# Low parts of weights: GpSimd's subtraction replaced by a negated copy on ScalarE and an adding DMA

## The chip, the cores and the metric

The kernel runs on one core of a Trainium2 chip. The metric is the device time of one execution in microseconds (us). The core's engines work side by side, each through its own queue in order: TensorE (PE in the rows; PEld is its weight load), VectorE (DVE), ScalarE (ACT), GpSimd (POOL) and SyncE (SP), which only issues DMAs. ScalarE and GpSimd can issue DMAs too.

## The reference

Linear attention with learned features, then two stacks of dense products. The second and third stage are what matters here:

```python
def _moe_ref(x, w_a, w_b, w_out):                    # x 1152x512, w_a and w_b 512x1536, w_out 1536x512
    return ((x @ w_a) * (x @ w_b)) @ w_out

def _moe2_ref(x, domain_probs, w1, w2):              # 4 experts, w1 512x1024, w2 1024x512 each
    p = domain_probs / (domain_probs.sum(-1, keepdims=True) + 1e-09)
    out = 0
    for e in range(4):
        out += p[:, e:e + 1] * (np.maximum(x @ w1[e], 0.0) @ w2[e])
    return out
```

Before that, phi(x) = exp of plus and minus (x @ w_phi less its largest magnitude); keys and values give sums per head, queries divide them out.

## The kernel before

TensorE multiplies in a rounded 32-bit format (float32r). To keep precision, each operand is cut into a high part, the rounded value, and a low part, what rounding took away; each product is then three matmuls: high by high, high by low, low by high. The low part of the *weight* is read by the third matmul of a product with stationary weights (lines 602, 686, 716, 743 and 772) and by the second where the weight moves (line 818).

**Where low parts are made.** `two_parts` (line 108): ScalarE rounds the source into `hi` (line 109), then GpSimd subtracts `hi` from the source into `lo` (line 110). It is called in two places, 116 times in all.
- `parts` (line 449), for the first MLP, 36 times, 128x512. Its weights (`ab` for the two inner products, `o` for the outer) come as 64-bit numbers. `begin` (ScalarE: two copies), `middle` (VectorE: lines 436, 439, 442; GpSimd: an integer addition, line 445) make 32-bit values in a tile `wx` of two buffers, and `parts` cuts them into `w`.
- `parts_w` (line 497), for the second MLP, 16 units of five calls. A unit ("1", j) has seven 256-column slices, made of sums of the loaded weights by a scheme that saves products (`sums_w`, GpSimd); they are cut in calls of 768, 512 and 512 columns into `wc`, of which there are two in turn. A unit ("2", j) has two calls of 512 columns into `w`.

**What sets the order.** The tasks `begin`, `middle`, `parts`, `load_w`, `sums_w` and `parts_w` stand in one list. `prep(n)` runs the next n of them, as long as the buffer that they write has had its last reader in program order; `need(u)` runs all that a unit of weights still lacks. During attention a string (`SCRIPT`, letter w) says where a task is run; after it `run` gives so many tasks for each step of matmuls. Nothing else moves them: each engine goes through its queue in the order of the program.

**Stages on the time line of the profile.** Attention to about 93 us; the first MLP, which begins inside it at 81 us, to about 328 us (units of 288 tokens, in its middle blocks of 384); then the second MLP, whose first unit begins between the first's last ones, in a regular pattern of about 24 us for each j from 346 us to the end.

Two lines are needed word for word. A product with the weight's low part in the third matmul, and the wait that VectorE's write of `wx` implies, since that tile has two buffers:

```python
nc.tensor.matmul(out=ps, lhsT=wlo, rhs=xhi, start=False, stop=a == 1, skip_group_check=True)     # line 602
x = w_p.tile([128, 512], U32, tag="wx", name="wx", bufs=2)                                       # line 434
```

Of the kernel before, what the change touches and what calls it, by code (L numbers as in the profile page):

```python
# [12 lines left out]
AF = mybir.ActivationFunctionType  # L13
ALU = mybir.AluOpType
# [40 lines left out]
def tile_linear_attention_then_mlps(ctx, tc, qT, kT, v, w_phi, wab, wout, w12, probs, out):  # L55
    nc = tc.nc
# [40 lines left out]
    with tc.manual_schedule():  # L97
# [10 lines left out]
        def two_parts(hi, lo, src, eng):  # L108
            nc.scalar.activation(out=hi, in_=src, func=AF.Copy)  # L109
            eng.tensor_tensor(out=lo, in0=src, in1=hi.bitcast(F32), op=ALU.subtract)  # L110

        NC = 6 * 128
        xraw = {}
# [300 lines left out]
        w_t = {}  # L414
        state = {}
# [33 lines left out]
        def parts(k):  # L449
            u, f = f64[k]  # L450
            if u in SPARE:
                if u not in w_t:
                    t = m_p.tile([128, 2, 2, 2, 512], F32R, tag="xc", name="w")
                    w_t.update((s, t[:, i]) for i, s in enumerate(SPARE))
            elif f == 0:
                p, n = (ab_p, 4) if u[0] == "ab" else (od_p, 2)
                w_t[u] = p.tile([128, 2, 2, 512], F32R, tag=u[0], name="w", bufs=n)
            two_parts(w_t[u][:, 0, f], w_t[u][:, 1, f], state.pop(k), nc.gpsimd)

        stage_t = {}  # L460

# [35 lines left out]
        def parts_w(u, lo, hi):  # L497
            def go():
                if u[0] == "1":
                    w_t[u] = wc_t[u[1] % 2]  # L500
                    src = stage_t[u][0][:, 1:4] if lo == 0 else stage_t[u][1][:, lo - 3:hi - 3]
                else:
                    src = stage_t[u][:, lo:hi]
                    if lo == 0:
                        w_t[u] = od_p.tile([128, 2, 2, 512], F32R, tag="o", name="w", bufs=2)
                two_parts(w_t[u][:, 0, lo:hi], w_t[u][:, 1, lo:hi], src, nc.gpsimd)
            return go


# [2 lines left out]
        for k in range(NW + 2):  # L512
            if k >= 2:
                tasks.append((f64[k - 2][0], lambda k=k: parts(k - 2), f64[k - 2][1] == 0))
            if 1 <= k <= NW:
                tasks.append((f64[k - 1][0], lambda k=k: middle(k - 1), False))
            if k < NW:
                tasks.append((f64[k][0], lambda k=k: begin(k), False))
# [261 lines left out]
        def unit_h(j, tp):  # L780
            c = new_c("h")

            def parts(src, f, lo, hi):
                free_hh(tp)
                nc.scalar.activation(out=hh_of(tp, f, 0, lo, hi), in_=src, func=AF.Relu)  # L785
                nc.vector.scalar_tensor_tensor(  # L786
                    out=hh_of(tp, f, 1, lo, hi), in0=src, scalar=0.0, in1=hh_of(tp, f, 0, lo, hi).bitcast(F32),
                    op0=ALU.max, op1=ALU.subtract,
                )

            def last(X):
                parts(X, 1, HT, 2 * HT)
                rows = range(4) if tp == 0 else range(4, 9)
                (queue if j + tp else kept).extend(
                    (pos[0] + (4 if j + 1 == tp else 3), ((0, 0, S), (1, 0, S)) if i == 4 else ((tp, 0, S),), lambda i=i: o2(j, i))
                    for i in rows
                )

            return unit(
                ("1", j), tp, c, lambda: parts(c[:, 0], 0, 0, 2 * HT), lambda: parts(c[:, 1, :HT], 1, 0, HT), last  # L800
            )
# [225 lines left out]
```

## Time and profile before

| | |
|---|---|
| median of 3 runs | 705.61 us (705.39 to 706.54) |
| the profiled execution, whole | 705.69 us |
| its span (first to last instruction) | 703.8 us |
| TensorE busy | 694.3 us, 99% |
| VectorE busy | 413.2 us, 59% |
| ScalarE busy | 295.5 us, 42% |
| GpSimd busy | 274.5 us, 39% |
| DMA, mean | 65 GB/s, 46.04 MB |

Times in rows count from the start of the span. A busy share is an average over the whole span and says nothing of a single stage; idle time of an engine on which nobody waits costs nothing. A matmul's row shows its start and a modelled end; neighbours overlap, so the distance of starts is what one costs. What an engine waited for is inferred from semaphores.

### The profile page before, as it was taken

What the parts mean: (1) busy time and instruction counts of PE and PEld (TensorE: products, weight loads), DVE (VectorE), ACT (ScalarE), POOL (GpSimd) and SP (SyncE); (2) the same over time, 40 slices, a digit from 0 to 9 for tenths busy, and PEclk for the clock granted to TensorE, in tenths of its full rate; (3) what the DMA queues carried; (4) which work ended last, traced back from release to release, by engine and by line L of the source; (5) the groups of instructions that cost most, each with busy time, mean ns of one, the idle gap of its engine ahead of it and who ended that gap; (6) DMA issues with size and microseconds to landing.
All of it is one profiled execution on the core that took longest, in us unless ns stands there. A gap on an engine that the chain in (4) does not pass through costs nothing.

```text
span 703.8 us, 13086 instructions
## 1 busy us (share of the span) xinstructions
PE 694.3 (99%) x5202; PEld 638.3 (91%) x5202; DVE 413.2 (59%) x721; ACT 295.5 (42%) x595; POOL 274.5 (39%) x242
## 2 busy tenths in 40 slices
PE   9998999999999999999999999999999999999998
PEld 8995689999999999999889898989898889888987
DVE  6899865657665565636345555555545554545454
ACT  6677855354434443335633243333323332333221
POOL 2222564334434437331763534353435243524200
PEclk9999999999999999999999999999999999999999
DMA  7641222313232321121221110211022101100003
GB/s 211 193 143 51 77 74 65 86 61 98 89 84 90 90 70 53 61 61 31 61 73 47 61 31 31 61 60 31 31 61 56 34 31 61 47 15 0 1 1 136
DMA packets 47966, 46.04 MB, mean 65 GB/s; under 512 B 5584, under 2 KB 39952, under 8 KB 47904
## 3 DMA queue, kind: packets, MB, share of 16 engines
q1 hardware_dynamic: 47648, 45.00, 21.5%
q8 instruction: 41, 0.67, 0.4%
q14 instruction: 21, 0.17, 0.1%
q10 hardware_dynamic: 224, 0.16, 0.1%
q0 software_dynamic: 32, 0.03, 0.0%
HBM read 42.81 MB, written 2.36 MB: 64 GB/s over the span
## 4 chain that ended last, share of the span: by engine, by line
PE 92%; DVE 5%; issue 1%; ACT 0%; POOL 0%; SPq 0%; DVEq 0%; ACTq 0%
PE acc L819 10%; PE acc L818 9%; PE acc L817 9%; PE X L600 5%; PE X L601 5%; PE X L602 5%; PE kv L237 5%; PE ab L685 4%; PE ab L684 4%; PE ab L686 4%; PE acc L715 2%; PE Z L600 2%; PE acc L716 2%; PE Z L601 2%; PE acc L714 2%; PE Z L602 2%
## 5 line engine op out<-in xcount | busy, mean ns | idle before, releaser
L827 DVE SCALAR_TENSOR_TENSOR oacc<-acc,pr,oacc 128x512 f32<-128x512 f32 (+1 forms) x136 | 101.4, 746 | 116.8 <-PE acc L819 116.8
L110 POOL TENSOR_TENSOR w<-wx,w 128x512 fp32r<-128x512 f32 x68 | 90.2, 1327 | 157.5 <-ACT w L109 157.5
L819 PE MATMUL acc<-w,hhb 128*128 128x512 f32 x290 | 114.1, 394 | 0.0
L818 PE MATMUL acc<-w,hhb 128*128 128x512 f32 x290 | 113.4, 391 | 0.0
L110 POOL TENSOR_TENSOR wc<-wt,wc 128x512 fp32r<-128x512 f32 (+1 forms) x48 | 69.9, 1482 | 110.3 <-ACT wc L109 110.0
L817 PE MATMUL acc<-w,hhb 128*128 128x512 f32 x290 | 112.9, 389 | 0.0
L445 POOL TENSOR_TENSOR wx<-wx,rn 128x512 uint32<-128x512 uint32 x36 | 46.4, 1289 | 95.9 <-DVE wx L442 95.9
L600 PE MATMUL X<-xc,wc 128*128 128x288 f32 x256 | 77.0, 301 | 0.7 <-ACT h L605 0.5
L785 ACT ACTIVATE hhb<-h 128x288 fp32r<-128x288 f32 x64 | 36.2, 565 | 98.2 <-DVE h L608 98.2
L601 PE MATMUL X<-xc,wc 128*128 128x288 f32 x256 | 75.8, 296 | 0.0
L685 PE MATMUL ab<-xl,w 128*128 128x288 f32 x256 | 75.5, 295 | 0.2 <-POOL xl L338 0.2
L684 PE MATMUL ab<-xh,w 128*128 128x288 f32 x256 | 75.6, 295 | 0.0
L686 PE MATMUL ab<-xh,w 128*128 128x288 f32 x256 | 75.4, 295 | 0.0
L602 PE MATMUL X<-xc,wc 128*128 128x288 f32 x256 | 75.4, 295 | 0.0
L605 ACT ACTIVATE h<-X 128x288 f32<-128x288 f32 x64 | 26.0, 406 | 108.5 <-PE X L602 108.4
L819 PEld LDWEIGHTS acc<-w,hhb 128*128 128x128 f32 x290 | 54.4, 188 | 14.0 <-DVE hhb L786 2.8
L786 DVE SCALAR_TENSOR_TENSOR hhb<-h,hhb 128x288 fp32r<-128x288 f32 x64 | 39.6, 618 | 42.2 <-ACT hhb L785 42.2
L818 PEld LDWEIGHTS acc<-w,hhb 128*128 128x128 f32 x290 | 54.4, 188 | 8.3
L817 PEld LDWEIGHTS acc<-w,hhb 128*128 128x128 f32 x290 | 54.5, 188 | 7.8
L608 DVE TENSOR_TENSOR part<-acc,part 128x288 f32<-128x288 f32 (+2 forms) x80 | 34.6, 451 | 33.4 <-PE acc L772 19.9
L600 PEld LDWEIGHTS X<-xc,wc 128*128 128x128 f32 x256 | 48.0, 188 | 4.3 <-ACT h L605 0.7
L601 PEld LDWEIGHTS X<-xc,wc 128*128 128x128 f32 x256 | 48.2, 188 | 2.7
(105 smaller groups left out, 1629.2 us busy)
## 6 DMA issues: line engine op xcount, KB each, us to landing
raw<-in_wab SPq DMA_DIRECT2D x192, 64.0 KB, 2.0
wt<-in_w SPq DMA_DIRECT2D x64, 128.0 KB, 2.4
wx<-in_w SPq DMA_DIRECT2D x32, 256.0 KB, 3.0
raw<-in_wout SPq DMA_DIRECT2D x12, 512.0 KB, 3.7
xraw<-in_qT SPq DMA_DIRECT2D x6, 384.0 KB, 3.4
v<-in_v SPq DMA_DIRECT2D x8, 256.0 KB, 4.6
out<-oacc SPq DMA_DIRECT2D x8, 256.0 KB, 2.0
xraw<-in_kT SPq DMA_DIRECT2D x4, 384.0 KB, 5.1
```

The costliest lines, as they stand in the source:

```text
L110: eng.tensor_tensor(out=lo, in0=src, in1=hi.bitcast(F32), op=ALU.subtract)
L445: nc.gpsimd.tensor_tensor(out=x, in0=x, in1=r, op=ALU.add)
L600: nc.tensor.matmul(out=ps, lhsT=whi, rhs=xhi, start=first and a == 0, stop=False, skip_group_check=True)
L601: nc.tensor.matmul(out=ps, lhsT=whi, rhs=xlo, start=False, stop=False, skip_group_check=True)
L602: nc.tensor.matmul(out=ps, lhsT=wlo, rhs=xhi, start=False, stop=a == 1, skip_group_check=True)
L684: nc.tensor.matmul(out=t, lhsT=whi, rhs=hi, start=(c == 0), stop=False)
L685: nc.tensor.matmul(out=t, lhsT=whi, rhs=lo, start=False, stop=False)
L686: nc.tensor.matmul(out=t, lhsT=wlo, rhs=hi, start=False, stop=(c == KD - 1))
L817: nc.tensor.matmul(out=acc, lhsT=hi, rhs=whi, start=f == 0, stop=False)
L818: nc.tensor.matmul(out=acc, lhsT=hi, rhs=wlo, start=False, stop=False)
L819: nc.tensor.matmul(out=acc, lhsT=lo, rhs=whi, start=False, stop=f == 1)
L827: nc.vector.scalar_tensor_tensor(out=o, in0=acc, scalar=sc, in1=o, op0=ALU.mult, op1=ALU.add)
```

## The change

`two_parts` stays, and nothing calls it any more. A new function takes its place at both calls. ScalarE rounds into `hi` as before, then writes the rounded value with its sign turned into `lo`; a DMA that GpSimd issues adds the source onto `lo`. So `lo` is again source minus rounded value. Seven lines come in at line 111, so line numbers of the changed kernel below it are higher by seven.

```diff
+        def two_parts_dma(hi, lo, src):
+
+
+            nc.scalar.activation(out=hi, in_=src, func=AF.Copy)
+            nc.scalar.activation(out=lo, in_=src, func=AF.Copy, scale=-1.0)
+            nc.gpsimd.dma_start(out=lo, in_=src, accum_op=ALU.add)
...
-            two_parts(w_t[u][:, 0, f], w_t[u][:, 1, f], state.pop(k), nc.gpsimd)
+            two_parts_dma(w_t[u][:, 0, f], w_t[u][:, 1, f], state.pop(k))
...
-                two_parts(w_t[u][:, 0, lo:hi], w_t[u][:, 1, lo:hi], src, nc.gpsimd)
+                two_parts_dma(w_t[u][:, 0, lo:hi], w_t[u][:, 1, lo:hi], src)
```

The queues of the built programs show what moved, at three places.

ScalarE's queue at the change-over to the second MLP, before. `wc` is the unit ("1", 1), `w` the unit ("2", 1), `wt` and `wx` their loaded sources; the lines between are copies out of PSUM:

```order
L605 ACTIVATE h<-X 128x288
L109 ACTIVATE wc<-wt 128x768
L605 ACTIVATE h<-Z 128x288
L785 ACTIVATE hhb<-h 128x288
L109 ACTIVATE wc<-wt 128x512
L785 ACTIVATE hhb<-h 128x576
L785 ACTIVATE hhb<-X 128x288
L109 ACTIVATE wc<-wt 128x512
L605 ACTIVATE h<-X 128x288
L109 ACTIVATE w<-wx 128x512 x2
```

And in the changed program:

```order
L612 ACTIVATE h<-X 128x288
L115 ACTIVATE wc<-wt 128x768
L116 ACTIVATE wc<-wt 128x768
L612 ACTIVATE h<-Z 128x288
L792 ACTIVATE hhb<-h 128x288
L115 ACTIVATE wc<-wt 128x512
L116 ACTIVATE wc<-wt 128x512
L792 ACTIVATE hhb<-h 128x576
L792 ACTIVATE hhb<-X 128x288
L115 ACTIVATE wc<-wt 128x512
L116 ACTIVATE wc<-wt 128x512
L612 ACTIVATE h<-X 128x288
```

Behind each rounding stands its negated copy (line 116), ahead of the copies that came next; nothing else changed its place.

GpSimd's queue in the first MLP's first weights, with its waits, before (`xl` is the low part of the input x, `rn` the rounding term of the 64-bit numbers):

```order
L110 TENSOR_TENSOR w<-wx,w 128x512 [waits Activation_49]
L445 TENSOR_TENSOR wx<-wx,rn 128x512 [waits DVE_49]
L338 TENSOR_TENSOR xl<-x,xh 128x576 [waits Activation_49]
L110 TENSOR_TENSOR w<-wx,w 128x512 [waits Activation_49]
L445 TENSOR_TENSOR wx<-wx,rn 128x512 [waits DVE_49]
```

And changed:

```order
L117 DMA w<-wx 128x512 [waits Activation_49,Pool_49]
L452 TENSOR_TENSOR wx<-wx,rn 128x512 [waits DMASW4_49,DVE_49]
L345 TENSOR_TENSOR xl<-x,xh 128x576 [waits Activation_49]
L117 DMA w<-wx 128x512 [waits Activation_49,Pool_49]
L452 TENSOR_TENSOR wx<-wx,rn 128x512 [waits DMASW5_49,DVE_49]
```

Each subtraction became a DMA at the same place. The addition to `wx` now also waits for the landing of an earlier adding DMA (DMASW is the completion of a DMA that GpSimd issued), that of two weights before, which read the same buffer; VectorE's write of `wx` (line 442, now 449) waits for it too, in place of a subtraction.

TensorE's queue where the second MLP's unit ("1", 0) begins, with its waits, before:

```order
L600 MATMUL X<-xc,wc 128x288 [waits Activation_49]
L601 MATMUL X<-xc,wc 128x288 [waits DVE_49]
L602 MATMUL X<-xc,wc 128x288 [waits Pool_49]
L600 MATMUL X<-xc,wc 128x288 [waits Activation_49]
L601 MATMUL X<-xc,wc 128x288 [waits DVE_49]
```

And changed:

```order
L607 MATMUL X<-xc,wc 128x288 [waits Activation_49]
L608 MATMUL X<-xc,wc 128x288 [waits DVE_49]
L609 MATMUL X<-xc,wc 128x288 [waits DMASW5_49]
L607 MATMUL X<-xc,wc 128x288 [waits Activation_49]
L608 MATMUL X<-xc,wc 128x288 [waits DVE_49]
```

The order is the same; the first matmul that reads a low part waits for a DMA's completion in place of GpSimd. So it is for all 116 low parts.

## Rows read from the trace of the kernel before

**Rows 1.** The page: busy time by engine, and the chain that ended last.

```profile
PE 694.3 (99%) x5202; PEld 638.3 (91%) x5202; DVE 413.2 (59%) x721; ACT 295.5 (42%) x595; POOL 274.5 (39%) x242
...
PE 92%; DVE 5%; issue 1%; ACT 0%; POOL 0%; SPq 0%; DVEq 0%; ACTq 0%
```

**Rows 2.** Busy time in a stretch; columns as in its first line.

```profile
core 0: us, PE busy (x) PEld busy (x) DVE busy (x) ACT busy (x) POOL busy (x), PEclk, DMA share, GB/s
47.00:680.00 633.00, 628.65 (x4352) 576.16 (x4349) 363.42 (x634) 259.74 (x526) 262.76 (x227) 1.00 0.18 55
```

**Rows 3.** Timeline, regular part: start us, us, engine, line, out<-in [idle before <-releaser].

```profile
409.74 0.84 ACT L109 ACTIVATE wc<-wt 128x768 fp32r<-128x768 f32 x1
...
432.40 0.29 PE L602 MATMUL X<-xc,wc 128*128 128x288 f32 x1
```

**Rows 4.** Timeline at the change-over to the second MLP, ScalarE and TensorE.

```profile
333.77 0.84 ACT L109 ACTIVATE wc<-wt 128x768 fp32r<-128x768 f32 x1
...
335.98 0.62 ACT L109 ACTIVATE wc<-wt 128x512 fp32r<-128x512 f32 x1
...
338.94 1.15 ACT L109 ACTIVATE w<-wx 128x512 fp32r<-128x512 f32 x2
...
336.94 0.29 PE L602 MATMUL X<-xc,wc 128*128 128x288 f32 x1
...
338.53 0.29 PE L602 MATMUL Z<-xc,wc 128*128 128x288 f32 x1
```

**Rows 5.** Timeline around the second block's output weights, ScalarE, VectorE, TensorE.

```profile
122.98 0.63 ACT L109 ACTIVATE w<-wx 128x512 fp32r<-128x512 f32 x1 [0.86 <-POOL wx L445]
...
125.52 0.42 DVE L436 TENSOR_SCALAR m<-m 128x512 f32<-128x512 f32 x1
...
127.31 0.29 PE L716 MATMUL acc<-hhb,w 128*128 128x288 f32 x1
```

**Rows 6.** Timeline around the first MLP's last weights, ScalarE and TensorE.

```profile
273.84 0.63 ACT L109 ACTIVATE w<-wx 128x512 fp32r<-128x512 f32 x1 [2.90 <-POOL wx L445]
...
278.69 0.30 PE L716 MATMUL acc<-hhb,w 128*128 128x288 f32 x1
...
251.84 0.63 ACT L109 ACTIVATE w<-wx 128x512 fp32r<-128x512 f32 x1 [2.37 <-POOL wx L445]
...
257.51 0.29 PE L686 MATMUL ab<-xh,w 128*128 128x288 f32 x1
```

**Rows 7.** The page, groups: count, busy us, mean ns, idle before <-releaser.

```profile
L110 POOL TENSOR_TENSOR w<-wx,w 128x512 fp32r<-128x512 f32 x68 | 90.2, 1327 | 157.5 <-ACT w L109 157.5
...
L110 POOL TENSOR_TENSOR wc<-wt,wc 128x512 fp32r<-128x512 f32 (+1 forms) x48 | 69.9, 1482 | 110.3 <-ACT wc L109 110.0
```

**Rows 8.** DMA issues: KB each, median us to landing; GpSimd's own, ns min/median/max.

```profile
wx<-in_w SPq DMA_DIRECT2D x32, 256.0 KB, 3.0
raw<-in_wout SPq DMA_DIRECT2D x12, 512.0 KB, 3.7
xraw<-in_qT SPq DMA_DIRECT2D x6, 384.0 KB, 3.4
...
ww<-in_w_phi ACTq DMA_DIRECT2D x1, 32.0 KB, 2.4
ww<-in_w_phi POOLq DMA_DIRECT2D x1, 32.0 KB, 2.8
...
L100 POOL DMA_DIRECT2D ww<-in_w_phi x1: 656/656/656, 1.2 to 1.2; - x1
```

**Rows 9.** Timeline around 88 us, and line 442's ns min/median/max.

```profile
84.08 0.62 ACT L109 ACTIVATE w<-wx 128x512 fp32r<-128x512 f32 x1
...
88.16 1.74 DVE L442 SCALAR_TENSOR_TENSOR wx<-raw,m 128x512 uint32<-128x512 uint32 x1
89.82 0.74 DVE L331 TENSOR_TENSOR x<-num,rb 128x576 f32<-128x576 f32 x1
...
85.24 7.97 PE L304 MATMUL num<-qp,kvz 128*32 128x288 f32 x128
...
L442 DVE SCALAR_TENSOR_TENSOR wx<-raw,m x36: 691/693/1741, 22.7 to 270.7; 128x512 uint32<-128x512 uint32 x36
```

## The prediction

> **What bounds the kernel now.** I read the busy shares first. TensorE is busy for 694.3 of 703.8 us and nothing else is above 59%; the chain that ended last is TensorE for 92% [rows 1]. Then the idle time: between 47 and 680 us TensorE is busy for 628.65 of 633 us, at full granted clock, so it idles for 4.35 us there [rows 2]. The kernel is a queue of matmuls with almost no hole. So an edit to the preparation of weights can gain very little, and the question is whether each weight still arrives before the matmul that reads it. The third matmul of each product is the first to read a low part; I measured, weight by weight, from the end of the rounding on ScalarE to that matmul. For most of the 116 weights this is above 10 us. In the regular part of the second MLP the rounding of a 768-column part starts at 409.74 us and its low part is read at 432.40 us [rows 3]. At a few places it is 2 to 5 us, and these carry the prediction [rows 4 to 6].
>
> **What goes.** 116 subtractions on GpSimd, 90.2 + 69.9 = 160.1 of its 274.5 us [rows 1, 7]. GpSimd was idle before most of them and is off the chain, so this alone saves nothing.
>
> **What comes on ScalarE.** 116 negated copies right behind the rounding. Two 512-column ones take 1.15 us together [rows 4], so the second adds 0.53 us beside 0.62 for one: 0.1 us overlaps. For 768 columns that leaves 0.84 - 0.1 = 0.74 us. With 68 + 32 of the first and 16 of the second: 100 x 0.53 + 16 x 0.74 = 65 us on an engine that is busy for 295.5 us. Behind each in ScalarE's queue stand copies out of PSUM; near the tight places ScalarE idles between them, so I cost this delay at nothing. If that cover were missing, a delay would be one copy, 0.5 to 0.7 us, at a time.
>
> **What comes on the queues.** 116 DMAs from GpSimd. The only DMA that GpSimd issues now, of 32 KB, holds it for 0.66 us [rows 8]; that is half a subtraction (1.33 us), so GpSimd's other work (line 445) is not later. The new waits: TensorE's third matmul waits for a landing instead of a subtraction; VectorE's write of wx (line 442) and GpSimd's addition to it wait until the DMA of two weights earlier has read that buffer; SyncE's later loads wait for the same landings, whose data are wanted tens of us later.
>
> **The price of a landing.** No row shows an adding DMA, nor one from SBUF to SBUF. Nearest rows [rows 8]: the same 32 KB takes 2.8 us from GpSimd and 2.4 us from ScalarE, so 0.4 us for the issuer; 256 KB from SyncE take 3.0 us and 512 KB take 3.7 us, so 0.7 us for each 256 KB more. An adding DMA has to read source and destination, for 256 KB of weight 512 KB: 3.7 + 0.4 = 4.1 us. For 384 KB it reads 768 KB: 3.7 + 0.7 + 0.4 = 4.8 us. I take these because bytes read is what sets the rows apart. Lower end: 2.8 us, and 0.4 more for 384 KB (3.4 against 3.0): 3.2 us. Upper end: two transfers one behind the other, 2 x 3.0 + 0.4 = 6.4 us and 2 x 3.4 + 0.4 = 7.2 us.
>
> **The sum, place by place.**
> - Change-over to the second MLP [rows 4]: the rounding of the 768 columns ends at 333.77 + 0.84 = 334.61 us, the negation at 335.35, the landing at 335.35 + 4.8 = 340.15. TensorE wants it at 336.94: **3.2 us late**. The next part is rounded at 335.98: 336.60, negated 337.13, landed 341.2; wanted at 338.53 + 3.2 = 341.7: in time.
> - Output weights of the second block of the first MLP [rows 5]: 122.98 + 0.63 + 0.53 + 4.1 = 128.24 against 127.31: **0.9 us late**.
> - Its last output weights [rows 6]: 273.84 + 0.63 + 0.53 + 4.1 = 279.1 against 278.69: **0.4 us late**. At 251.84 the same chain ends at 257.1, against 257.51: in time.
> - VectorE's wx [rows 9]: the weight rounded at 84.08 is negated by 85.23 and lands at 89.3; line 442 would wait from 88.16, 1.2 us. But there it takes 1.74 us instead of the usual 0.69, beside a subtraction that goes. So the x behind it (89.82 now) moves by about 0.2 us, to an end at 90.7; TensorE wants its PSUM for the last of four groups of num, at 85.24 + 3 x 1.99 = 91.2. Nothing.
> - The regular part [rows 3]: 409.74 + 0.84 + 0.74 + 4.8 = 416.1 against 432.40. Nothing, and hidden by 16 us.
>
> TensorE has no idle time later in which to win this back, so the delays add: 3.2 + 0.9 + 0.4 = 4.5 us. The profiled execution took 705.69 us, of which 703.8 are the span; that is 0.08 above the median of the runs (705.61). 705.7 + 4.5 = **710.2 us**.
>
> **A rule weighed.** VectorE's max/min on m (line 436) starts at 125.52 us [rows 5], 1.4 us after the adding DMA would be issued at 124.14, and twice the 0.66 us that GpSimd's one DMA holds it now [rows 8]; so the sum has no term for it. The Trainium skill, "SBUF — State Buffer", section "SBUF: two separate sides", speaks against this change: a DMA from GpSimd is held up while VectorE runs in a mode that uses both its ports, since GpSimd cannot write descriptors then. If the descriptors took past 125.52 us, the sum by that rule would grow by the 0.42 us of that row, to 710.6 us. No run here shows it.
>
> **The rivals.**
> - *A longer landing, 6.4 and 7.2 us.* The add is a second pass over the data. Against it: the engines are little used (DMA share 0.18 [rows 2]). Then 335.35 + 7.2 - 336.94 = 5.6; 124.14 + 6.4 - 127.31 = 3.2; 275.0 + 6.4 - 278.69 = 2.7; 253.0 + 6.4 - 257.51 = 1.9; and wx lands at 91.6, x ends at 91.6 + 0.69 + 0.74 = 93.1 against 91.2, 1.9 [rows 4, 5, 6, 9]. Sum 15.3: 721.0 us. Chance 0.22, and 0.05 more for a landing still longer, at which the waits on wx spread.
> - *A shorter landing, 2.8 and 3.2 us.* For it: no HBM is read. Only the change-over is left, 335.35 + 3.2 - 336.94 = 1.6: 707.3 us. Chance 0.17, of which 0.07 at or under 0.2%. The Trainium skill, "DMA: Bandwidth & Descriptors", section "Anatomy of one DMA — SWDGE (gpsimd) path", fits a DMA from GpSimd by 2.0 us plus bytes over 436 GB/s; an estimate by it is 2.9 us for 384 KB, so 1.3 us late and 707.0 us. It is silent on additions, and no run here shows it yet.
> - *Faster.* Without subtractions, VectorE's operations that ran beside them shorten (1.74 to 0.69 us at 88.16 [rows 9]) and TensorE's small waits close. At most the 4.35 us of idle time [rows 2]: 701.3 us. It decides only if the change-over costs nothing, with a landing within 336.94 - 335.35 = 1.6 us; none of the landings shown is under 2.4 us [rows 8]. Chance 0.03.
> - *No effect*: the low parts come in time in a way that I don't see. That the edit isn't carried out I exclude: the order of the built program has the DMAs in place of the subtractions. Chance 0.03, at 705.7 us.
>
> **How the numbers follow.** The forecast has 0.50, the long landings 0.27, the short 0.17, faster 0.03, none 0.03. Slower by over 0.2% (1.4 us, about what a measurement of this kernel can tell from no change): 0.50 + 0.27 + 0.10 = 0.87; within 0.2%: 0.07 + 0.03 = 0.10; faster: 0.03. The range goes from a little under the short landing, 706.8, to the long one with 2 us for weights whose slack lies between those summed, 723; outside are the still longer landings, faster and none, 0.11, and the ends of the two landings.
>
> **What would show it.** TensorE waiting for a DMA on wc near 337 us for about 3 us, and for 0.4 to 1 us near 127 and 279 us; GpSimd's busy time down to 115 us, ScalarE's up to 360 us; landings of 4 to 5 us in the list of DMA issues; the stretch from 346 to 680 us as long as before. I am wrong if landings are above 6 us or under 3 us, if the regular part gets longer, or if TensorE waits for PSUM copies of ScalarE.

## The result and the profile after

The changed kernel takes 713.17 us (median of 4 executions, 711.72 to 713.97) against 705.56 us before (705.39 to 706.54): a ratio of 1.0103, 95% interval 1.009 to 1.0115. So it is 7.6 us slower; 4.5 us were forecast, and the time lies inside the range.

The profiled execution is the shortest of the four: 711.72 us, span 709.9, 6.1 us more than before. That leaves two questions: where these 6.1 us are, and why the others took up to 2.3 us more.

Engines and chain on the page of the changed kernel, to hold against [rows 1]:

```profile
PE 695.4 (98%) x5202; PEld 638.4 (90%) x5202; DVE 402.8 (57%) x721; ACT 357.7 (50%) x711; POOL 217.0 (31%) x242
...
PE 87%; DVE 6%; ACT 2%; issue 2%; DMA 2%; POOL 1%; SPq 0%; DVEq 0%; ACTq 0%; POOLq 0%
```

ScalarE went up by 62.2 us (65 forecast). DMA and ScalarE are new in the chain. GpSimd's 217.0 us count the issue of its DMAs as busy, 0.87 us each in the page's groups; without these two groups they are 115.8 (115 forecast):

```profile
L117 POOL DMA_DIRECT2D w<-wx x68 | 59.6, 876 | 209.8 <-DMA wt<-in_w 65.6
...
L117 POOL DMA_DIRECT2D wc<-wt x48 | 41.6, 873 | 138.1 <-ACT h L612 115.6
```

The landings, in the list of DMA issues (KB each, median us from issue to landing):

```profile
w<-wx POOLq DMA_DIRECT2D x68, 256.0 KB, 3.4
...
wc<-wt POOLq DMA_DIRECT2D x32, 256.0 KB, 4.3
...
wc<-wt POOLq DMA_DIRECT2D x16, 384.0 KB, 4.0
```

Next the stretches of [rows 2], which I split at 346 us; first the changed kernel:

```profile
47.00:346.00 299.00, 290.25 (x2381) 272.32 (x2378) 180.07 (x340) 164.94 (x324) 103.86 (x100) 1.00 0.45 106
346.00:680.00 334.00, 333.50 (x1936) 298.34 (x1935) 171.13 (x290) 154.84 (x315) 102.51 (x128) 1.00 0.50 104
```

The kernel before, same stretches:

```profile
47.00:346.00 299.00, 294.82 (x2413) 277.27 (x2410) 188.62 (x341) 146.16 (x286) 127.91 (x105) 1.00 0.25 72
346.00:680.00 334.00, 333.83 (x1941) 298.89 (x1940) 174.81 (x294) 113.59 (x241) 134.85 (x122) 1.00 0.13 39
```

In the regular part TensorE is as full as before (333.50 of 334 us), although the DMA share there went from 0.13 to 0.50. All that was lost was lost ahead of 346 us. Who made TensorE wait between 80 and 130 us (total, times, longest):

```profile
PE acc L723 <- DMA w<-wx: 0.4, 1, 0.4
PE num L311 <- ACT den L321: 0.4, 1, 0.4
```

And between 250 and 345 us:

```profile
PE X L609 <- DMA wc<-wt: 1.8, 1, 1.8
PE acc L722 <- DVE hhb L704: 1.0, 2, 0.6
PE acc L721 <- ACT hhb L612: 0.9, 1, 0.9
PE Z L607 <- ACT h L612: 0.7, 1, 0.7
```

None of these was there before. Setting the n-th matmul of each line against the same matmul of the kernel before shows the steps by which TensorE falls behind; a step is a little longer than its wait, as the first matmul behind a wait takes 0.40 us in place of 0.29. They are the six places of the table, named by the time of that matmul in the kernel before; in the changed kernel it comes later by the steps so far.

| us in the kernel before | step | TensorE waits for |
|---|---|---|
| 89 | 0.6 | a copy of ScalarE (line 321) behind a late rounding and a negation |
| 127 | 0.7 | the landing of an output weight's low part |
| 259 | 1.7 | a copy of ScalarE (line 612) behind a late load |
| 279 | 0.9 | a product of VectorE (line 704) beside GpSimd's sums |
| 335 | 0.7 | a copy of ScalarE (line 612) behind a negation |
| 337 | 2.1 | the landing of the 768-column low part |

Their sum is 6.7 us; the last matmul is 6.1 us behind, so 0.6 us are won back elsewhere, half of it near 165 us. Two of the six, 2.8 us, are landings. The expectations further down use an earlier reading of the same steps: 0.5, 0.6, 1.7, 0.8, 0.85 and 2.0 us.

At 89 us two delays meet. ScalarE's rows, the kernel before and then the changed one:

```profile
87.36 0.63 ACT L109 ACTIVATE w<-wx 128x512 fp32r<-128x512 f32 x1 [0.28 <-POOL wx L445]
87.90 0.63 ACT L314 ACTIVATE den<-num 128x576 f32<-128x576 f32 x1
```

```profile
87.89 0.63 ACT L115 ACTIVATE w<-wx 128x512 fp32r<-128x512 f32 x1 [1.00 <-POOL wx L452]
...
88.95 0.63 ACT L321 ACTIVATE den<-num 128x576 f32<-128x576 f32 x1
```

The rounding begins 0.53 us later, because GpSimd's addition (line 452), which it waits for, ends at 87.85 us in place of 87.32; the negation between the two adds 0.52. So the copy `den` is 1.05 us later.

The change-over, in the timeline of the changed kernel (against [rows 4]):

```profile
337.31 0.84 ACT L115 ACTIVATE wc<-wt 128x768 fp32r<-128x768 f32 x1
...
338.05 0.83 ACT L116 ACTIVATE wc<-wt 128x768 fp32r<-128x768 f32 x1
...
338.78 0.40 ACT L612 ACTIVATE h<-Z 128x288 f32<-128x288 f32 x1
339.18 0.88 POOL L117 DMA_DIRECT2D wc<-wt  x1 [8.97 <-ACT h L612]
...
339.23 0.40 PE L607 MATMUL Z<-xc,wc 128*128 128x288 f32 x1 [0.67 <-ACT h L612]
...
343.19 0.40 PE L609 MATMUL X<-xc,wc 128*128 128x288 f32 x1 [1.83 <-DMA wc<-wt]
```

The negation ends at 338.88. The DMA starts 0.30 us later and lands 3.96 us after that, at 343.14. Ahead of it, the copy of Z, which had stood right behind the rounding, runs behind the negation, and TensorE, which wants that buffer free, waits 0.67 us for it.

Near 259 us, timeline of the changed kernel:

```profile
254.47 0.87 POOL L117 DMA_DIRECT2D w<-wx  x1 [1.73 <-ACT w L116]
...
259.37 0.66 ACT L435 ACTIVATE m<-raw 128x512 f32<-128x512 f32 x1 [3.71 <-DMA raw<-in_wab]
...
260.49 0.67 ACT L612 ACTIVATE hhb<-gg 128x576 fp32r<-128x576 f32 x1
...
261.21 0.40 PE L721 MATMUL acc<-hhb,w 128*128 128x288 f32 x1 [0.90 <-ACT hhb L612]
```

ScalarE stands before `begin` of a later weight, whose load has not landed, and the copy of the product `gg` (line 612), which TensorE needs now, is queued behind it. The last piece of that load was issued at 254.6 us, 0.14 us behind the adding DMA, and took 4.7 us; before it took 2.9. The same line's instructions in that stretch, changed kernel and then before:

```profile
L413 SPq DMA_DIRECT2D raw<-in_wab x1: 1193/1193/1193, 254.6 to 254.6; - x1
...
DMA to landing us min/median/max: 4.7/4.7/4.7
```

```profile
L406 SPq DMA_DIRECT2D raw<-in_wab x1: 1311/1311/1311, 253.7 to 253.7; - x1
...
DMA to landing us min/median/max: 2.9/2.9/2.9
```

The Trainium skill, "DMA: Bandwidth & Descriptors", section "SWDGE vs HWDGE vs iDMA", says that DMAs from GpSimd and those from other queues feed different queues inside each DMA engine, which takes them in turn. That agrees with these rows: the load is held up though the two were issued by different engines.

Near 279 us VectorE's product took 2.65 us, while GpSimd's four sums ran; before, the same product took 0.80 us, also beside them (timelines of the changed kernel and then of the kernel before):

```profile
278.85 3.66 POOL L499 TENSOR_TENSOR wt<-wt 128x256 f32<-128x256 f32 x4
...
279.27 2.65 DVE L704 TENSOR_TENSOR hhb<-gg,hhb 128x576 fp32r<-128x576 f32 x1 [0.75 <-ACT hhb L612]
```

```profile
275.80 3.47 POOL L492 TENSOR_TENSOR wt<-wt 128x256 f32<-128x256 f32 x4
...
276.35 0.80 DVE L697 TENSOR_TENSOR hhb<-gg,hhb 128x576 fp32r<-128x576 f32 x1 [0.75 <-ACT hhb L605]
```

### The profile page after: what moved, and what is told of

Read it like the earlier page. It is cut to its first block, busy times and chain, and to the rows that moved or that the text cites. A ratio compares the mean times of both kernels' runs of the same rounds, so it can differ in the third digit from the quotient of the medians.

```text
span 709.9 us, 13406 instructions
## 1 busy us (share of the span) xinstructions
PE 695.4 (98%) x5202; PEld 638.4 (90%) x5202; DVE 402.8 (57%) x721; ACT 357.7 (50%) x711; POOL 217.0 (31%) x242
## 4 chain that ended last, share of the span: by engine, by line
PE 87%; DVE 6%; ACT 2%; issue 2%; DMA 2%; POOL 1%; SPq 0%; DVEq 0%; ACTq 0%; POOLq 0%
PE acc L826 9%; PE acc L825 9%; PE acc L824 9%; PE X L607 5%; PE X L609 5%; PE X L608 5%; PE kv L244 4%; PE ab L692 4%; PE ab L691 4%; PE ab L693 4%; PE acc L722 2%; PE acc L723 2%; PE Z L608 2%; PE Z L607 2%; PE Z L609 2%; PE acc L721 2%
## 5 line engine op out<-in xcount | busy, mean ns | idle before, releaser
L117 POOL DMA_DIRECT2D w<-wx x68 | 59.6, 876 | 209.8 <-DMA wt<-in_w 65.6
L117 POOL DMA_DIRECT2D wc<-wt x48 | 41.6, 873 | 138.1 <-ACT h L612 115.6
L452 POOL TENSOR_TENSOR wx<-wx,rn 128x512 uint32<-128x512 uint32 x36 | 48.1, 1337 | 78.6 <-DVE wx L449 78.6
L499 POOL TENSOR_TENSOR wt<-wt 128x256 f32<-128x256 f32 x64 | 51.4, 985 | 1.3
L607 PEld LDWEIGHTS X<-xc,wc 128*128 128x128 f32 x256 | 48.0, 188 | 4.0 <-ACT h L612 0.7
```

The costliest lines, as they stand in the source:

```text
L117: nc.gpsimd.dma_start(out=lo, in_=src, accum_op=ALU.add)
L499: nc.gpsimd.tensor_tensor(out=o, in0=i, in1=j, op=op)
L607: nc.tensor.matmul(out=ps, lhsT=whi, rhs=xhi, start=first and a == 0, stop=False, skip_group_check=True)
```

## The experiments

Three theories stood against each other: **A**, late data at the six places; **B**, ScalarE's 62 us of added copies delay everything a little; **C**, landings alone, as predicted. Where a version uses subtraction for some weights, it calls `two_parts` of the kernel before for them.

**First and second MLP apart.**

First MLP alone, in `parts_w`:

```diff
-                two_parts_dma(w_t[u][:, 0, lo:hi], w_t[u][:, 1, lo:hi], src)
+                two_parts(w_t[u][:, 0, lo:hi], w_t[u][:, 1, lo:hi], src, nc.gpsimd)
```

> Adding DMAs for the 36 weights of the first MLP alone; the second MLP's low parts by GpSimd's subtraction as before. Theory A (late data at six places: in the changed kernel TensorE's matmuls shift by 0.5 us near 89, 0.6 near 127, 1.7 near 259, 0.8 near 279, 0.85 near 335 and 2.0 us near 337): the first four stay, 3.6 us, so 709.2 us; 708.4 if the 0.8 near 279 is an accident between VectorE and GpSimd. Theory B (ScalarE's 65 us of added copies delay everything a little; 20 us of them are in the first MLP): about 36/116 of 7.6 us, 2.4 us, 708.0. Theory C (landings alone, as predicted): 0.6 us, 706.2.

Second MLP alone, in `parts`:

```diff
-            two_parts_dma(w_t[u][:, 0, f], w_t[u][:, 1, f], state.pop(k))
+            two_parts(w_t[u][:, 0, f], w_t[u][:, 1, f], state.pop(k), nc.gpsimd)
```

> Adding DMAs for the 80 calls of the second MLP alone; the first MLP's low parts by subtraction. Theory A: 0.85 near 335 and 2.0 near 337, 2.85 us, so 708.4. Theory B: 80/116 of 7.6 us, 5.2 us, 710.8. Theory C: 2.8 us all at 337 (without the delay of a copy near 335 the landing is wanted earlier), 708.4. First and second alone add up to the change if nothing else is at work.

Measured: first alone 710.42 us, 1.0063 (1.0051 to 1.0076), +4.4; second alone 709.64, 1.0042 (1.0028 to 1.0056), +3.6 (before, in that session: 706.01). The sum, 8.0, is the change's 7.6. C falls with the first MLP (+0.6 expected), and B's split, 2.4 and 5.2, is the wrong way round. A is nearest, but both are above it by 0.8 us. In the traces the steps at 89, 127, 259 and 279 us, and at 335 and 337, are there as in the changed kernel, but behind the largest one the matmuls themselves are longer, for 3.41 us, at a granted clock of 0.5. The changed kernel's own profile had no such stretch; more on it below. For the second MLP alone the executions divide by it: the two with a mean granted clock of 1.000 took 707.79 and 708.26 us, the three with 0.998 took 709.64 to 709.81. For the first MLP alone the clock does not account for the rest: its median execution, 710.42 us, has a mean clock of 1.000 and no trace, so what it lost beyond A is not shown.

**The addition by GpSimd in place of the DMA.**

```diff
-            nc.gpsimd.dma_start(out=lo, in_=src, accum_op=ALU.add)
+            nc.gpsimd.tensor_tensor(out=lo, in0=src, in1=lo.bitcast(F32), op=ALU.add)
```

> ScalarE's negated copies stay; GpSimd adds the source by an instruction in place of each DMA. Theory A: only the copies behind a negation stay late, 0.85 near 335 and 0.4 near 89, so 706.8; the landing near 337, near 127 and the late load near 259 are gone. Theory B: nearly the whole 7.6 us stay, 712 or more. Theory C: 705.6.

Measured: 707.46 us, 1.002 (1.0011 to 1.0029), +1.45. TensorE's waits between 80 and 345 us:

```profile
PE Z L607 <- ACT h L612: 0.7, 1, 0.7
PE num L311 <- ACT den L321: 0.5, 1, 0.5
PE acc L722 <- DVE hhb L704: 0.4, 1, 0.4
```

ScalarE's copies alone keep the two steps at 89 and 335 us (0.7 us each here). The other 6 us come with the DMAs. B has fallen.

**The negation ahead of the rounding.**

```diff
-            nc.scalar.activation(out=hi, in_=src, func=AF.Copy)
             nc.scalar.activation(out=lo, in_=src, func=AF.Copy, scale=-1.0)
+            nc.scalar.activation(out=hi, in_=src, func=AF.Copy)
```

> The negated copy runs ahead of the rounding, so each DMA is issued earlier by one copy, 0.53 us for 512 columns and 0.74 for 768; the rounded value is later by as much. Theory A: near 127 the 0.6 us become 0.1, near 337 the 2.0 become 1.25; 0.85 near 335 and 1.7 near 259 stay (the load meets the DMA as before): 713.2 less 1.3, 711.9. Theory B: 713.2, no change. Theory C: each loss at a landing falls by one copy, the same 1.3 us.

Measured: 711.40 us, 1.0083 (1.0069 to 1.0096). Between 120 and 345 us TensorE waits for:

```profile
PE acc L721 <- ACT hhb L612: 1.3, 1, 1.3
PE X L609 <- DMA wc<-wt: 1.1, 1, 1.1
PE acc L722 <- DVE hhb L704: 0.8, 2, 0.4
PE Z L607 <- ACT h L612: 0.7, 1, 0.7
```

The wait at 337 us fell by 0.7 us, one copy of 768 columns, and the one at 127 us is gone: the two losses at landings are the chain of rounding, negation and landing. ScalarE's 0.7 us at 335 stayed. The 1.3 us are not where they were expected: the matmul that waited stands at 168 us in this trace, behind ScalarE's wait for another late load.

```profile
166.15 0.67 ACT L435 ACTIVATE m<-raw 128x512 f32<-128x512 f32 x1 [4.20 <-DMA raw<-in_wab]
```

In the changed kernel this wait of ScalarE's was 2.72 us, and TensorE lost nothing there; near 259 us the step is 0.8 us here in place of 1.7. So which late load costs something, and how much, differs between executions, and the six places of the table are those of one execution. The interval of the ratio overlaps that of the change, and the clock shows as fallen (mean 0.998) in one execution of four here and in two of four there; so the traces tell of the two landings, not the time.

**One weight by subtraction.** In `parts`, all else as changed:

```diff
-            two_parts_dma(w_t[u][:, 0, f], w_t[u][:, 1, f], state.pop(k))
+            (two_parts_dma if k != 31 else lambda a, b, c: two_parts(a, b, c, nc.gpsimd))(w_t[u][:, 0, f], w_t[u][:, 1, f], state.pop(k))
```

> One of the 116 weights, the 32nd of the first MLP, whose adding DMA is issued at 254.5 us beside the last piece of a raw load, is made by subtraction again; all else as in the changed kernel. Theory A (that DMA holds up the load, ScalarE waits for the load, and the copy for the output product stands behind it): the piece lands in about 2.9 us in place of 4.65, ScalarE's line 435 starts about 1.7 us earlier, and the step of 1.3 + 0.4 us at 259 is gone; the time falls by 1.7 us, and by up to 1.7 more where a fall of the clock behind that stall went with it. Rival (the load was late for another reason, or ScalarE's queue is late by its copies alone): at most 0.5 us less.

Measured: 712.00 us, 1.0089 (1.0075 to 1.0102). In the trace the load's last piece lands in 2.0 us, and between 255 and 265 us TensorE waits for nothing. All of this stretch runs 1.7 us later here, as this execution lost more ahead of it (below, on the place near 38 us):

```profile
L413 SPq DMA_DIRECT2D raw<-in_wab x1: 427/427/427, 257.3 to 257.3; - x1
...
DMA to landing us min/median/max: 2.0/2.0/2.0
```

The 2.0 us do not compare as they stand, since this piece was issued 1.5 us behind the piece before it, in place of 0.47. From the issue of the piece before to the landing of the last it is 3.5 us here, 3.4 in the kernel before, 5.1 in the changed kernel and 5.4 with the first MLP alone, where the adding DMA stands beside it as well (there the piece took 4.9 us). So that one adding DMA held up the load, by 1.6 us. TensorE's step near 259 us is 0.1 us here; as up to 0.65 us stand there in a trace without that DMA too (three calls only, negation first, below), not all of the 1.7 us need be its doing. In the medians it shows as 1.2 us less, but the intervals of the two ratios overlap; the traces carry the verdict, not the time.

**A DMA that copies and does not add.**

```diff
-            nc.gpsimd.dma_start(out=lo, in_=src, accum_op=ALU.add)
+            nc.gpsimd.dma_start(out=lo, in_=src)
```

> The DMA copies the source over the negated value in place of adding to it: the addition is left out, and with it the reading of the destination. If bytes read set the landing, as the prediction priced it, 0.7 us less for 256 KB and 1.1 less for 384 KB: 2.6 and 2.9 us in place of 3.3 and 4.0. If the addition costs nothing, 3.3 and 4.0 stay, and the time stays within 1 us of the changed kernel.

This version leaves the addition out, so its low parts hold the source itself. Measured: 709.92 us, 1.0057 (1.0043 to 1.007). Its landings in the list of DMA issues:

```profile
w<-wx POOLq DMA_DIRECT2D x68, 256.0 KB, 2.3
...
wc<-wt POOLq DMA_DIRECT2D x16, 384.0 KB, 2.6
```

And how long an issue holds GpSimd (line 117's instructions, ns min/median/max):

```profile
L117 POOL DMA_DIRECT2D w<-wx x68: 527/546/605, 27.9 to 664.9; - x68
```

The addition, with the reading of the destination that goes with it, costs 1.1 us of landing for 256 KB (3.4 against 2.3), 1.4 for 384 KB (4.0 against 2.6), and 0.33 us more of GpSimd's time for each issue. It grows with the bytes, as the prediction priced it, and is larger than the 0.7 and 1.1 us expected. The wait at 337 us is 0.5 us here. Of the 4.1 us that stay, the steps in this trace are 0.9 us by 45 us, 0.3 at 89, 0.6 near 165, 0.65 near 259, 0.7 at 335 and 0.8 at 337: with shorter landings, most of what is left is no landing.

**Three calls only.** The first MLP by subtraction, as above, and in `parts_w` the adding DMA for the unit ("1", 1) alone; in a second version also with the negation first.

```diff
-                two_parts_dma(w_t[u][:, 0, lo:hi], w_t[u][:, 1, lo:hi], src)
+                (two_parts_dma if u == ("1", 1) else lambda a, b, c: two_parts(a, b, c, nc.gpsimd))(w_t[u][:, 0, lo:hi], w_t[u][:, 1, lo:hi], src)
```

> Three of 116 calls, those of the unit (1, 1), by adding DMA, all others by subtraction. Theory A: 0.85 near 335 and 2.0 near 337, so before + 2.85 us, and 1.7 more in executions in which the clock falls behind the stall, as it did with the second MLP alone. If the other 77 calls of the second MLP cost something, this is under the second MLP alone (+3.6 us) by that.

> Three of 116 calls by adding DMA, those of the unit (1, 1), with the negated copy ahead of the rounding. Theory A: the wait near 337 falls from 1.8 to 1.1 us, the 0.85 near 335 stays: before + 2.1 us with the clock up; if the clock falls behind the shorter wait too, + 3.8. In the version with the rounding first it fell in five of five executions. Rival (that version's +4.1 us was stall alone): +3.4 here, with the clock up.

Measured: rounding first 709.95 us, 1.006 (1.0046 to 1.0073), +4.1; negation first 708.02, 1.0033 (1.002 to 1.0045), +2.2. Three calls of 116 cost as much as all 80 of the second MLP (+3.6). With the rounding first all five executions had a mean granted clock of 0.998; with the negation first none (0.999 to 1.000). The stretches around the wait, rounding first:

```profile
338.00:340.62 2.62, 0.85 (x7) 0.81 (x7) 1.13 (x2) 1.77 (x4) 1.43 (x2) 1.00 0.95 169
340.62:344.03 3.41, 3.41 (x14) 3.22 (x14) 0.46 (x1) 1.86 (x4) 2.61 (x3) 0.50 0.55 96
```

TensorE had stood idle for 1.77 us up to 339.81, and 0.8 us later its granted clock is at 0.50, 1.2 GHz, for 3.41 us. At half the clock that costs 3.41 / 2 = 1.7 us: 0.7 + 2.0 + 1.7 = 4.4 us. At the end this execution's matmuls are 4.6 us behind, 0.2 of which were lost ahead of 335 us. The negation first: 1.1 us of wait, no fall, 2.2 us in the median.

**The tight places back.** Subtraction for the unit ("1", 1) and the first MLP's weights 6, 7, 12, 32 and 36; in a second version for weights 1 to 5 too. In `parts` of the first, with `k > 6 and k not in (11, 31, 35)` in the second:

```diff
-            two_parts_dma(w_t[u][:, 0, f], w_t[u][:, 1, f], state.pop(k))
+            (two_parts_dma if k not in (5, 6, 11, 31, 35) else lambda a, b, c: two_parts(a, b, c, nc.gpsimd))(w_t[u][:, 0, f], w_t[u][:, 1, f], state.pop(k))
```

> Eight of 116 calls by subtraction, the others by adding DMA: the unit (1, 1) (335 and 337), and the first MLP's weights 6 and 7 (near 89), 12 (near 127), 32 (near 259) and 36 (near 279). Theory A: all six losses go, before + 0 to 0.5 us. A cost spread over all DMAs or copies: 108/116 of 7.6 us, before + 7 us.

> As the version with eight calls by subtraction, but also the first MLP's weights 1 to 5, which are made during attention: 13 of 116 calls by subtraction, 103 by adding DMA. There the eight-call version lost its remaining 1 us: near 37 us ScalarE's copies of keys stand behind a negation after a late load. Theory A: before + 0 to 0.4 us; not faster than before, since TensorE has nothing left to win. Rival (the remaining 1.3 us of that version is spread over the 103 DMAs): before + 1.1 us.

Measured: eight calls back 707.13 us, 1.0017 (1.0008 to 1.0026); thirteen back 705.47, 0.9994 (0.9985 to 1.0003), against 705.85 and 705.86 of before. The first missed its expectation by 0.8 us. Its trace has no wait of TensorE between 250 and 345 us, but one near 38 us that is not in the kernel before:

```profile
PE kv L244 <- ACT kp L220: 0.3, 1, 0.3
```

There ScalarE, in the timeline of that version, comes out of a wait for a load at 35.04 us and then works without a gap; the negation at 37.19 stands ahead of the copy of the keys:

```profile
35.04 0.67 ACT L435 ACTIVATE m<-raw 128x512 f32<-128x512 f32 x1 [3.01 <-DMA v<-in_v]
...
37.19 0.62 ACT L116 ACTIVATE w<-wx 128x512 fp32r<-128x512 f32 x1
37.71 0.61 ACT L220 ACTIVATE kp<-r 128x512 f32<-128x512 f32 x1
```

How much is lost there differs between the traces: by 45 us the matmuls are 1.6 us behind in this one, 1.8 with the negation first, 1.4 with one weight back, 0.9 with the copying DMA, and at most 0.4 in the others, that of the changed kernel among them. What makes the load late in some executions is not shown.

With these weights back too, nothing is lost. 103 of the 116 adding DMAs cost nothing, and bring nothing: TensorE's busy time between 47 and 680 us is that of [rows 2] (628.65), with GpSimd at 211.18 us in place of 262.76:

```profile
47.00:680.00 633.00, 628.83 (x4354) 576.32 (x4352) 355.58 (x634) 315.88 (x630) 211.18 (x227) 1.00 0.45 100
```

This is no version that beats both kernels.

## Why the prediction was right, and where it was wrong

- **The time lies in the range, in part by luck.** Its mechanism, TensorE waiting for landings, is there, but it makes 2.8 of the 6.7 us of steps; the other 3.9 us come at places for which the sum had nothing, or a landing instead. The range reached above 710.2 us for the sake of longer landings and of weights with little slack; it came to hold losses of another kind. One of the signs of being wrong that the prediction named, TensorE waiting for PSUM copies of ScalarE, did appear, at 89 and 335 us.
- **Direction, bound and regular part: right.** TensorE is the bound, the regular part hides every landing (the longest of all took 6.2 us), GpSimd's time is worth nothing. Thirteen calls back undo the whole loss.
- **Change-over, 3.2 us forecast: 2.8 measured, of another make.** "The landing at 335.35 + 4.8" took 0.30 + 3.96 = 4.26 us, shorter by 0.5. But 0.7 us of the loss is ScalarE's copy of Z behind the negation. The step at the low part itself is then 2.1.
- **127 us, 0.9 forecast: 0.7.** The negation ended at 124.08, the DMA started at 124.63 and landed at 128.38: 4.3 us. The sum had 4.1; the rest is slack that TensorE's loss at 89 us had added.
- **279 us, 0.4 forecast: no wait for the landing.** It came at 281.59 us, 0.6 ahead of the matmul that reads it, as that was late itself. The 0.9 us there are VectorE's product beside GpSimd's sums, which the sum did not have. With the first MLP alone the product took 2.65 us again, with the negation first 1.41: how the two engines meet decides it. The Trainium skill, "SBUF — State Buffer", section "SBUF: two separate sides", says that a VectorE instruction with two inputs in SBUF contends with a GpSimd instruction that reads it. The 2.65 us agree with that; the 0.80 us of the kernel before, beside the same sums, show that they need not delay each other.
- **"Near the tight places ScalarE idles between them, so I cost this delay at nothing": the step that failed first.** The cover was missing at 89 and 335 us, and near 38 us in executions with a late load. The version without DMAs puts the price of all added copies at 1.45 us. The prediction looked at the places where landings were tight, and not at the copies on which TensorE waits behind each negation. ScalarE's queue, quoted ahead, has the copy of Z right behind the negation at the change-over; whether TensorE waits for that buffer was not looked up.
- **"So GpSimd's other work (line 445) is not later": wrong at 89 us.** The DMA started 0.55 us behind the negation, at 85.67 us, where the subtraction had started at 84.78, and the addition behind it ended 0.53 us later. That is half of what delayed the copy there.
- **"SyncE's later loads wait for the same landings, whose data are wanted tens of us later": the step that failed most.** 1.7 us at 259. It isn't the wait of a load for a landing, it is a load in flight beside an adding DMA, and ScalarE's queue standing before that load. The prediction weighed contention only for the landing itself, by the mean DMA share of 0.18.
- **The wx of line 442: the wait came as worked out** (1.23 us, 1.2 forecast; the adding DMA issued at 85.67 us landed at 89.67; the x behind it began 0.6 us later, not 0.2), and cost nothing: without the DMAs the loss at 89 us stayed.
- **The Trainium skill's rule that the prediction weighed, that VectorE holds up GpSimd's descriptors:** at 127 us the issue took 0.88 us, the median is 0.87; no delay shows there. The landing took 3.75 us against a median of 3.4; whether VectorE has a part in that is not shown.
- **The copying fit:** an estimate by the Trainium skill's 2.0 us plus bytes over 436 GB/s ("DMA: Bandwidth & Descriptors", section "Anatomy of one DMA — SWDGE (gpsimd) path") is 2.6 and 2.9 us. The copies landed in 2.3 and 2.6, the adding DMAs in 3.4 and 4.0. It holds roughly for copies, and not for additions.
- **What lies between the profile's 6.1 us and the median's 7.6:** in part the clock. Of the changed kernel's four executions two had a mean granted clock of 1.000 (711.72 and 712.63 us) and two 0.998 (713.71 and 713.97); 3.41 us at half the clock are 1.7 us, and the two pairs lie 1.7 us apart. The 0.9 us between the first two are not explained; the second has no trace. The prediction has no term for the clock. That it fell at the change-over in those two isn't shown, as they have no trace; in the traces that have a fall it stood behind the waits at 259 or 337 us.

## What to carry to other kernels

When work moves off an engine that nobody waits for, what counts is the slack of each single consumer at the places where the queue is tight; an average share hides them, and here the whole loss went with 13 of 116 calls. Count three things for each moved step: the new latency to its reader, the instructions that now stand behind the added one in its engine's queue, and the transfers that are in flight beside an added DMA. On a kernel that keeps TensorE full, a wait of some 2 us may cost 1.7 us more by the clock behind it, so shortening such a wait can be worth more than its length: here 0.7 us less of wait at the change-over won 1.9 us (+4.1 against +2.2).

## What the runs showed of the hardware

- An adding DMA from GpSimd between two tiles of SBUF lands 3.2 us after its issue at best (256 KB), 3.4 to 4.3 us in the median, 4.0 us for 384 KB, and 6.2 at the longest; the same DMA as a copy lands in 2.3 and 2.6. GpSimd is held for 0.87 us by the one and 0.55 by the other, and starts it mostly 0.30 to 0.55 us after the end of the ScalarE instruction that it waits for.
- A load of 64 KB issued 0.14 us behind such a DMA landed after 4.7 us in place of 2.9, and after 4.9 in a second version; counted from the issue of the piece before it, 5.1 and 5.4 us against 3.4, and 3.5 once that DMA was gone.
- TensorE's clock fell to 1.2 GHz for 3.41 us behind a wait of 1.77 us in five of five executions of one kernel (by the mean granted clock; one of them traced), and in none of five where the wait was 1.1 us. Behind a wait of 1.83 us in the traced execution of the changed kernel it did not fall.
